# Two expert units computed by token halves during attention, the gate's maximum on TensorE, looser joins, and a decode load issued ahead

## The chip, the cores and the metric

The kernel runs on one NeuronCore of a Trainium2 chip. The metric is device time in microseconds of one launch. Five engines run side by side, each with its own queue in order: PE (TensorE, matmuls into PSUM banks), DVE (VectorE), ACT (ScalarE), POOL (GpSimd) and SP (SyncE, which here only issues DMAs). They meet through semaphores.

## The reference

Attention over 4 batches, 8 heads and 576 positions (four heads with a local window of 32, four with a stride of 32), then a mixture of 8 experts whose gate is normalised over all tokens, then an FFN whose int64 view of float64 weights is decoded on the chip:

```python
x = attention(q, k, v)                       # [2304, 512]: tokens x model
logits = x @ w_gate                          # [2304, 8]
P = np.exp(logits - logits.max())            # one maximum over all tokens and experts
for _ in range(8):                           # Sinkhorn: rows, then columns
    P /= P.sum(1, keepdims=True) + 1e-09
    P /= P.sum(0, keepdims=True) + 1e-09
    P *= N / E
for e in range(8):
    out += P[:, e:e+1] * (np.maximum(x @ w1[e], 0) @ w2[e])
h = out @ w_in
y = (h / (1 + np.exp(-1.702 * h))) @ w_out
```

## The kernel before, in words

Tokens are taken in 3 blocks of 768. A *unit* is one slice of 256 hidden columns of an expert (4 units an expert) or of the FFN (8 units) for one block. There are 120 units in six phases: experts on block 0 (32 units), experts on block 1, FFN on block 0, experts on block 2, FFN on blocks 1 and 2.

Every fp32 operand is split into a high part (ScalarE, `Copy` to fp32r) and a low part (source minus high part, on GpSimd or VectorE), and a product is three matmuls (high·high, high·low, low·high) for each of two 128-row halves of the contraction: six matmuls of 384 columns (line 601). The 2×2 block product of a unit (two token halves of 384, two model halves, two column halves) would be 8 such products; `PRODUCTS` (line 39) does it in 7, with sums of the weights (T1 to T4, made on GpSimd, lines 190 to 192) and of the inputs (S1 to S4, lines 311 to 317). For that the sums of all four input quarters must be there, so both token halves of a block. The results are put together in PSUM banks A, B and C by ScalarE copies (`copy_of`, line 612) and VectorE adds (`add`, line 640; line 658), then `activate` makes the hidden values hh (ScalarE) and hl (VectorE, line 624). `tile_down` multiplies 128 tokens by w2, six matmuls of 512 columns into y (lines 678 to 680), and adds y to the accumulator on VectorE (lines 691 to 707).

The program is a list of *pieces*: 13 a unit, a product and a tile_down in turn (the tile_down is that of the unit before). `side[n]` holds what else is issued after piece n: weight splits, input splits (`plan_inputs`), gate steps, the decode of FFN weights, joins. `advance()` issues the next piece with its side work. All engines' queues are filled in this one order.

The attention comes first, in 48 groups of queries through a pipeline of 52 steps (`att_step`): in step i the groups i-4 (values, line 469), i-3 (transpose, line 451), i-1 (exp) and i (scores, line 400) take their turn, with three gaps a step on PE. In steps 0 to 23 the gaps hold matmuls on zeros (`keep_warm`, line 787; 1.5 a gap on average). Before step 24 the first inputs are put together (`combine`: sum, high, low, all in a row), and from there each gap advances 1.3 pieces (`RATE`). Attention groups write x through VectorE (lines 479, 489).

The probabilities are known only after the whole attention, so the first three experts (`WAITING`) are added up unweighted, stored, and joined later (`plan_kept`, line 721): load at units 14, 17, 20, and six joins of 128 tokens within 18 pieces each. After the attention the gate steps run, one after each piece: logits, maximum over a partition (line 550), maximum over the partitions (`partition_all_reduce` on GpSimd, line 551), exp, 8 Sinkhorn rounds (each with a matmul by ones, line 571). The step behind the last one starts the decode: load (line 259) and 8 VectorE operations (lines 260 to 269) a chunk, 32 chunks spread to unit 60.

What the units of block 0 split is stored to DRAM (s1moe, s2moe) and loaded again for blocks 1 and 2.

Of the kernel before, what the change touches and what calls it, by code (L numbers as in the profile page):

```python
# [15 lines left out]
P = 128  # L16
# [9 lines left out]
NH = 384  # L26
# [6 lines left out]

RATE = 1.3

# [16 lines left out]
def strided_attention_moe_ffn(  # L52
# [130 lines left out]

    def sums_w1(i):

        r = raw[1, i]
        t = rawp.tile([P, 4, 2 * P], F32, tag="sums", name="sums")
# [8 lines left out]
    WHERE = {"W11": (1, 0), "W21": (1, 2), "W22": (1, 3), "T1": (3, 0), "T3": (3, 1), "T2": (3, 2), "T4": (3, 3)}  # L196

    def split_w1(i, k):
        what = PRODUCTS[k][1]
        t = w1p.tile([P, 2, 2 * P], F32R, tag="w1", name="w1")  # L200
        _, kind, blk, n = UNITS[i]
        kept = sw1[kind][n, k].rearrange("p (h c) -> p h c", h=2)
        w1[i, k] = t
        if blk:
            nc.sync.dma_start(out=f(t), in_=kept)
            return
        which, q = WHERE[what]
        src = raw[which, i][:, q, :]
        nc.scalar.activation(out=t[:, 0, :], in_=src, func=AF.Copy)  # L209
        nc.gpsimd.tensor_tensor(out=t[:, 1, :], in0=src, in1=f(t[:, 0, :]), op=ALU.subtract)  # L210
        nc.sync.dma_start(out=kept, in_=f(t))

    def split_w2(i, ft):
        t = w2p.tile([P, 2, D], F32R, tag="w2", name="w2")
        _, kind, blk, n = UNITS[i]
        kept = sw2[kind][n, ft].rearrange("p (h c) -> p h c", h=2)
        w2[i, ft] = t
        if blk:
            nc.sync.dma_start(out=f(t), in_=kept)
            return  # L220
        src = raw[2, i][:, ft, :]
        nc.scalar.activation(out=t[:, 0, :], in_=src, func=AF.Copy)  # L222
        nc.gpsimd.tensor_tensor(out=t[:, 1, :], in0=src, in1=f(t[:, 0, :]), op=ALU.subtract)  # L223
        nc.sync.dma_start(out=kept, in_=f(t))

    def plan_weights():

        for i in range(NU):
            new = [u < NU and UNITS[u][2] == 0 for u in range(i, i + 3)]

            if i + 1 < NU:
# [7 lines left out]
            for ft in range(2):  # L239
                side[piece_at(i, 4 + 2 * ft)].append(lambda i=i, ft=ft: split_w2(i, ft))  # L240
            if new[1]:
                side[piece_at(i, 7)].append(lambda i=i: load_w2(i + 1))


# [74 lines left out]
    def input_of(ph, m):  # L319
        what = PRODUCTS[m][0]  # L320
        return xin[SUMS[what], ph] if what in SUMS else quarters(ph)[what]

    def input_high(ph, m):
        if ph == 0 and not xc:
            xc.update({(0, n): xcp.tile([P, 2, 2, NH], F32R, tag="xc", name="xc") for n in range(NPR)})
        t = xc[0, m] if ph == 0 else xcp.tile([P, 2, 2, NH], F32R, tag="xc", name="xc")
# [6 lines left out]

    def combine(ph, m):

        input_sum(ph, m, nc.vector)
        input_high(ph, m)
        input_low(ph, m, nc.vector)
# [121 lines left out]
    def att_values(i, b, pair, g):  # L460
        eT, U, R, C = att.pop((b, pair, g))
        vt = att_in["v", b, pair]
        if i < NFIRST and i % 2:
            av = ps.tile([P, 512], F32, tag="C", name="av")
        else:
            av = eps.tile([P, 512], F32, tag="pa", name="av")
# [81 lines left out]
    def gate_max():  # L548
        mx = sk[:, 0, 0:1]
        nc.vector.tensor_reduce(out=mx, in_=pr, axis=AX.XY, op=ALU.max)  # L550
        nc.gpsimd.partition_all_reduce(sk[:, 0, 1:2], mx, P, bass.bass_isa.ReduceOp.max)

    def gate_exp():
        ng = sk[:, 0, 2:3]
        nc.vector.tensor_scalar_mul(ng, sk[:, 0, 1:2], -1.0)
        nc.scalar.activation(out=pr, in_=pr, func=AF.Exp, bias=ng)

# [34 lines left out]
    def product(i, k):  # L592
        ph, kind, blk, n = UNITS[i]
        _, _, b, opens, ends = PRODUCTS[k]
        if opens:
            open_bank(b, i)
        o = bank[b][:, :NH]
        w, x = w1.pop((i, k)), xc[ph, k]
        todo = [(kk, hw, hx) for kk in range(2) for hw, hx in ((0, 0), (0, 1), (1, 0))]
        for m, (kk, hw, hx) in enumerate(todo):  # L600
# [110 lines left out]
    def plan_kept():  # L711
# [43 lines left out]
    def unit_pieces(i):  # L755
        out = []
        for k in range(NPR):
            if i < NU:
                def prod(i=i, k=k):
                    r = product_and_after(i, k)  # L760
                    if r is not None:
                        later.append(r)
                out.append(prod)
            if k < TB:
                def down(i=i, k=k):
                    if i > 0:
                        tile_down(i - 1, k)
                    after()
                out.append(down)
        return out  # L770

    for i in range(NU + 1):
        pieces += unit_pieces(i)
# [5 lines left out]
    with tc.manual_schedule():  # L779
# [33 lines left out]

        quota = [0.0]
        ahead = {10 + 2 * k: (lambda k=k: split_w1(0, k)) for k in range(NPR)}
        ahead[9] = lambda: [t() for t in sums_w1(0)]
        load_w1(1)
        first = {13: 3, 17: 0, 22: 6}

        def fill_first():  # L820
            quota[0] += IDLE_GAP
            keep_warm(int(quota[0]))
            quota[0] -= int(quota[0])

        def fill():
            quota[0] += RATE
            while quota[0] >= 1:
                advance()
                quota[0] -= 1

        for i in range(NSTEP):
            if i < NFIRST + 4:
                att_step(i, fill_first)
                if i in ahead:
                    ahead[i]()
                if i in first:
                    combine(0, first[i])
            else:
                if i == NFIRST + 4:
                    combine(0, 1)  # L840
                    combine(0, 2)
                    side[2].append(lambda: combine(0, 4))
                    side[4].append(lambda: combine(0, 5))
                    side[PPU].append(lambda: gate_logits(0))
                att_step(i, fill)
        early.close()
# [92 lines left out]
```

## Time and profile before

| | us |
|---|---|
| three runs | 2064.30 median, 2060.92 to 2064.44 |
| profiled execution, its own time | 2064.13 |
| its span (first to last instruction) | 2062.3 |
| PE busy | 2023.6 (98%) |
| DVE / ACT / POOL busy | 1310.8 / 705.4 / 608.1 |
| mean granted TensorE clock | 0.993 of 2.4 GHz |

A row of the profile gives the line of the kernel, the engine, the operation and output<-inputs. Matmul durations overlap, so the cost of a matmul group is read from its start to the start of what follows. Windows and timelines are in us from the span's start.

### The profile page before, as it was taken

How to read it: one execution, taken by the hardware profiler on the slowest of the kernel's cores; microseconds unless marked ns; L12 is line 12 of the kernel's file. 1: busy time of each engine (PE TensorE's matmuls, PEld its weight loads, DVE VectorE, ACT ScalarE, POOL GpSimd, SP SyncE). 2: the span in 40 equal slices, each digit the busy share in tenths (PEclk: the TensorE clock that was granted, in tenths of full speed). 3: DMA queues.
4: the chain of work that ended last, by engine and by line, in shares of the span. 5: the costliest groups of instructions: out<-in, count | busy, mean ns of one | idle time of the engine just before them, and what ended most of it. 6: DMA issues, size and time to landing. Idle time of an engine off the chain costs nothing.

```text
span 2062.3 us, 30239 instructions
## 1 busy us (share of the span) xinstructions
PE 2023.6 (98%) x10538; PEld 1778.3 (86%) x10538; DVE 1310.8 (64%) x2310; ACT 705.4 (34%) x1735; POOL 608.1 (29%) x609
## 2 busy tenths in 40 slices
PE   9799999999999999999999999999999999999999
PEld 6577878888888888898898888888898889889888
DVE  6766576888778666666665666544554455466656
ACT  5655533443443222222222555222222222333432
POOL 3556656777777000000000667100000000300300
PEclk9899999999999999999999999999999999999999
DMA  5467567888887666666666676655555555655653
GB/s 182 145 217 279 205 237 268 314 305 300 282 289 250 205 206 228 220 213 220 223 209 201 215 244 209 219 180 189 187 179 185 198 177 181 194 180 178 209 190 128
DMA packets 185287, 445.51 MB, mean 216 GB/s; under 512 B 21040, under 2 KB 21168, under 8 KB 184368
## 3 DMA queue, kind: packets, MB, share of 16 engines
q1 hardware_dynamic: 184848, 443.12, 64.3%
q8 instruction: 84, 1.38, 0.3%
q14 instruction: 67, 0.55, 0.1%
q10 hardware_dynamic: 288, 0.46, 0.1%
HBM read 310.33 MB, written 133.17 MB: 215 GB/s over the span
## 4 chain that ended last, share of the span: by engine, by line
PE 87%; DVE 6%; issue 2%; DMA 2%; ACT 1%; POOL 1%; POOLq 0%; ACTq 0%; SPq 0%; DVEq 0%
PE pA L601 22%; PE y L680 15%; PE y L678 15%; PE y L679 15%; PE pC L601 11%; PE pB L601 5%; DMA acc<-kept 1%; PE sc L400 1%; PE idle_out L787 1%; PE av L469 1%; PE pt L451 1%; DVE acc L697 1%; POOL w L210 1%; DVE hl L634 1%; DVE xc L332 1%
## 5 line engine op out<-in xcount | busy, mean ns | idle before, releaser
L697 DVE SCALAR_TENSOR_TENSOR acc<-y,pr,acc 128x512 f32<-128x512 f32 x486 | 364.3, 750 | 445.7 <-PE y L680 443.0
L680 PE MATMUL y<-w,hl 128*128 128x512 f32 x1440 | 573.4, 398 | 5.7 <-DVE hl L624 3.7
L678 PE MATMUL y<-w,hh 128*128 128x512 f32 x1440 | 568.1, 395 | 6.9 <-DVE acc L693 3.8
L679 PE MATMUL y<-w,hh 128*128 128x512 f32 x1440 | 569.3, 395 | 0.0
L601 PE MATMUL pA<-xc,w 128*128 128x384 f32 x2880 | 565.0, 337 | 2.4 <-ACT c L612 1.7
L601 PEld LDWEIGHTS pA<-xc,w 128*128 128x128 f32 x2880 | 513.6, 189 | 37.0 <-ACT c L612 2.1
L680 PEld LDWEIGHTS y<-w,hl 128*128 128x128 f32 x1440 | 270.3, 188 | 68.0 <-DVE hl L624 6.3
L678 PEld LDWEIGHTS y<-w,hh 128*128 128x128 f32 x1440 | 270.8, 188 | 47.8 <-DVE acc L693 4.1
L679 PEld LDWEIGHTS y<-w,hh 128*128 128x128 f32 x1440 | 270.5, 188 | 33.5
L601 PE MATMUL pC<-xc,w 128*128 128x384 f32 x1440 | 294.4, 339 | 0.0
L601 PEld LDWEIGHTS pC<-xc,w 128*128 128x128 f32 x1440 | 258.9, 189 | 21.1 <-issue 0.6
L621 ACT ACTIVATE hh<-pB 128x384 fp32r<-128x384 f32 x192 | 94.5, 492 | 410.8 <-DVE pB L640 238.5
L612 ACT ACTIVATE c<-pA 128x384 f32<-128x384 f32 x240 | 117.6, 490 | 254.6 <-PE pA L601 254.6
L332 POOL TENSOR_TENSOR xc<-z,xc 128x768 fp32r<-128x768 f32 x8 | 15.1, 1891 | 546.0 <-ACT xc L327 546.0
L270 POOL TENSOR_TENSOR x<-x,r 128x512 f32<-128x512 f32 x32 | 41.4, 1294 | 415.7 <-DVE r L269 394.1
L601 PE MATMUL pB<-xc,w 128*128 128x384 f32 x720 | 145.8, 337 | 0.0
L210 POOL TENSOR_TENSOR w<-sums,w 128x256 fp32r<-128x256 f32 x160 | 126.8, 796 | 59.6 <-ACT w L209 52.4
L601 PEld LDWEIGHTS pB<-xc,w 128*128 128x128 f32 x720 | 128.1, 188 | 11.0 <-issue 0.5
L707 DVE TENSOR_TENSOR acc<-y,acc 128x512 f32<-128x512 f32 x126 | 86.4, 686 | 79.1 <-PE y L680 78.8
L223 POOL TENSOR_TENSOR w<-raw,w 128x512 fp32r<-128x512 f32 x80 | 107.1, 1339 | 85.4 <-ACT w L222 85.4
L612 ACT ACTIVATE c<-pC 128x384 f32<-128x384 f32 x120 | 59.0, 492 | 176.6 <-PE pC L601 176.6
L621 ACT ACTIVATE hh<-pC 128x384 fp32r<-128x384 f32 x96 | 47.2, 492 | 180.6 <-DVE pC L640 176.4
(109 smaller groups left out, 1995.7 us busy)
## 6 DMA issues: line engine op xcount, KB each, us to landing
w<-s1moe SPq DMA_DIRECT2D x448, 256.0 KB, 2.7
w<-s2moe SPq DMA_DIRECT2D x128, 512.0 KB, 3.7
s1moe<-w SPq DMA_DIRECT2D x224, 256.0 KB, 3.8
s2moe<-w SPq DMA_DIRECT2D x64, 512.0 KB, 3.8
w<-s1ffn SPq DMA_DIRECT2D x112, 256.0 KB, 2.7
raw<-wa SPq DMA_DIRECT2D x32, 512.0 KB, 4.9
raw<-wb SPq DMA_DIRECT2D x32, 512.0 KB, 5.3
w<-s2ffn SPq DMA_DIRECT2D x32, 512.0 KB, 3.8
```

The costliest lines, as they stand in the source:

```text
L210: nc.gpsimd.tensor_tensor(out=t[:, 1, :], in0=src, in1=f(t[:, 0, :]), op=ALU.subtract)
L223: nc.gpsimd.tensor_tensor(out=t[:, 1, :], in0=src, in1=f(t[:, 0, :]), op=ALU.subtract)
L270: lambda: nc.gpsimd.tensor_tensor(out=x, in0=x, in1=f(r), op=ALU.add),
L332: eng.tensor_tensor(out=t[:, 1], in0=input_of(ph, m), in1=f(t[:, 0]), op=ALU.subtract)
L601: nc.tensor.matmul(out=o, lhsT=w[:, hw, kk * P : (kk + 1) * P], rhs=x[:, hx, kk, :], start=opens and m == 0, stop=ends and m == len(todo) - 1,
L612: nc.scalar.activation(out=t, in_=bank[b][:, :NH], func=AF.Copy)
L621: nc.scalar.activation(out=hh, in_=src, func=AF.Relu)
L678: nc.tensor.matmul(out=y, lhsT=hh[:, c], rhs=w[:, 0], start=(m == 0), stop=False)
L679: nc.tensor.matmul(out=y, lhsT=hh[:, c], rhs=w[:, 1], start=False, stop=False)
L680: nc.tensor.matmul(out=y, lhsT=hl[:, c], rhs=w[:, 0], start=False, stop=(m == 1))
L697: nc.vector.scalar_tensor_tensor(out=a, in0=y, scalar=p, in1=a, op0=ALU.mult, op1=ALU.add)
L707: nc.vector.tensor_tensor(out=a, in0=y, in1=a, op=ALU.add)
```

## The change

1. The first two units (`PLAIN = 2`) take the plain 8 products with unsummed weights and inputs, token half by token half: half 0 of unit 0, half 0 of unit 1, half 1 of unit 0, half 1 of unit 1 (`half_pieces`, 4 products each, and the three tile_downs of the half before). Half 0 needs 384 tokens only. Its 11 pieces are issued from attention step 14 on, 0.4 a gap, one matmul on zeros in a gap without a piece.
2. From step 24 on the rate is 1.15 pieces a gap (1.3 before). Input sums and splits of unit 2 are side work of pieces 12 to 26; the splits of the plain quarters follow steps 10, 13, 22 and 23. Attention groups 6 to 11 are reordered. From group 11 on transposes go to bank `pa`, from group 10 to 19 values to bank B.
3. T1 to T4 of units 0 and 1, which blocks 1 and 2 still read, are made and stored later (`plan_sums`, units 16 to 27).
4. The gate's maximum over partitions: a matmul by the identity, a VectorE maximum, a matmul by ones.
5. Joins: loads at units 14, 19, 24, six joins within 52 pieces each. First decode load 8 pieces ahead of its use.
6. In the last unit before blocks 1 and 2, three low parts of inputs go from VectorE to GpSimd (`low_v`).

```diff
-RATE = 1.3
+RATE_HALF = 0.4
+RATE = 1.15
+PLAIN = 2
...
+        for at, k in zip((10, 12, 14, 16, 18, 19, 21), range(NPR)):
+            side[at].append(lambda k=k: split_w1(PLAIN, k))
+        side[8].append(lambda: [t() for t in sums_w1(PLAIN)])
...
+    def plan_sums(dp, i, lo, hi):
...
+        def split(k):
+            t = dp.tile([P, 2, 2 * P], F32R, tag="kw", name="kw", bufs=2)
+            split_into(t, quarter(i, PRODUCTS[k][1]), sw1["moe"][UNITS[i][3], k].rearrange("p (h c) -> p h c", h=2))
+        tasks = [load, lambda: None, sums] + [lambda n=n: r["todo"][n]() for n in range(4)]
+        tasks += [lambda k=k: split(k) for k in range(NPR) if PRODUCTS[k][1][0] == "T"]
+        spread(tasks, lo, hi)
...
+        side[lo - 8].append(lambda: step(0, 0))
         for i in range(len(todo)):
-            if i == 0:
-                order.append((0, 0))
...
+    def plan_first_sums():
+        v, g = nc.vector, nc.gpsimd
+        for m, at, eng in ((1, 12, g), (2, 17, v), (4, 21, g), (5, 25, v)):
+            side[at].append(lambda m=m: input_sum(0, m, v))
+            side[at + 1].append(lambda m=m, eng=eng: split_input(m, eng))
...
-            low_v = (1, 3, 5) if shared else (0, 3, 6) if PHASES[ph - 1][1] == 0 else ()
+            low_v = (1, 3, 5) if shared else ()
...
-        nc.gpsimd.partition_all_reduce(sk[:, 0, 1:2], mx, P, bass.bass_isa.ReduceOp.max)
+    def gate_max_row():
+        pm = spare_bank([P, 512], "pm")
+        nc.tensor.matmul(out=pm[:1, :P], lhsT=sk[:, 0, 0:1], rhs=ident, start=True, stop=True)
+        nc.vector.tensor_reduce(out=sk[:1, 0, 1:2], in_=pm[:1, :P], axis=AX.X, op=ALU.max)
+    def gate_max_all():
+        pm = spare_bank([P, 512], "pm")
+        nc.tensor.matmul(out=pm[:, :1], lhsT=ones[:1, :], rhs=sk[:1, 0, 1:2], start=True, stop=True)
+        nc.vector.tensor_scalar_mul(sk[:, 0, 2:3], pm[:, :1], -1.0)
...
-        steps += [lambda: None] * 3 + [gate_exp]
+        steps += [lambda: None, gate_max_row, lambda: None, gate_max_all, lambda: None, gate_exp]
...
+    HALVES = [(i, h) for h in range(2) for i in range(PLAIN)]
+    def half_product(n, k):
+        i, h = HALVES[n]
+        col, first = divmod(k, 2)
+        if not first:
+            open_bank("AC"[col], 0)
+        w = w1[i, ("W11", "W12")[col] if first else ("W21", "W22")[col]]
+        x = xc[0, (0, "X21")[h] if first else (3, 6)[h]]
+        o = bank["AC"[col]][:, :NH]
+        sum_of_six(o, w, x, not first, bool(first))
+        if first:
+            return activate(i, f"{h + 1}{col + 1}", o, f"{n % 2 + 1}{col + 1}")
...
-            u = WAITING * UPE + 2 + 3 * e
+            u = WAITING * UPE + 2 + 5 * e
-            spread([lambda e=e, t=t: join(e, t) for t in range(TB)], piece_at(u, 8), piece_at(u + 2, 0))
+            spread([lambda e=e, t=t: join(e, t) for t in range(TB)], piece_at(u, 8), piece_at(u + 4, 8))
...
+        def fill_half():
+            quota[0] += RATE_HALF
+            if quota[0] >= 1 and done[0] < BY_HALF:
+                advance()
+                quota[0] -= 1
+            else:
+                keep_warm(1)
```

Three places where the order moves. First PE in attention steps 17 and 18, before: av are values of a group, pt its transposes, sc scores, idle_out the matmuls on zeros.

```order
L469 MATMUL av<-eT,vt 64x72 x2
L787 MATMUL idle_out<-idle 128x384
L451 MATMUL pt<-cst,e 126x126 x4
L787 MATMUL idle_out<-idle 128x384 x2
L400 MATMUL sc<-qkt 96x128 x4
L787 MATMUL idle_out<-idle 128x384
```

The same place on PE in the changed kernel: pA<-xc,w is one half product, the six y rows are one tile_down.

```order
L515 MATMUL av<-eT,vt 64x72 x2
L657 MATMUL pA<-xc,w_544 128x384 x6
L495 MATMUL pt<-cst,e 126x126 x4
L887 MATMUL idle_out<-idle 128x384
L444 MATMUL sc<-qkt 96x128 x4
L750 MATMUL y<-w_456,hh_659 128x512
L751 MATMUL y<-w_456,hh_659 128x512
L752 MATMUL y<-w_456,hl_660 128x512
L750 MATMUL y<-w_507,hh_737 128x512
L751 MATMUL y<-w_507,hh_737 128x512
L752 MATMUL y<-w_507,hl_738 128x512
```

Of the 30 gaps of steps 14 to 23, 11 hold a piece (8 products, 3 tile_downs) and the others one matmul on zeros; before, each held 1 or 2 of these.

Second, GpSimd at the gate's maximum, before: the all-reduce (sk) stands between the weight splits (L210, L223) and the weight sums (L190) of two units.

```order
L223 TENSOR_TENSOR w_3090<-raw_2898,w_3090 128x512
L210 TENSOR_TENSOR w_3123<-raw_2805,w_3123 128x256
L551 ISA
L551 ISA sk<-sk 128x1
L210 ISA
L210 TENSOR_TENSOR w_3151<-sums,w_3151 128x256
L190 TENSOR_TENSOR sums<-raw_3013 128x512
```

In the changed kernel GpSimd has nothing of the gate, and PE has two small matmuls (pm) instead, a tile_down and a product apart.

```order
L657 MATMUL pA<-xc,w_2785 128x384 x6
L602 MATMUL pm<-cst,sk 1x128
L750 MATMUL y<-w_2773,hh_2900 128x512
L751 MATMUL y<-w_2773,hh_2900 128x512
L752 MATMUL y<-w_2773,hl_2901 128x512
L750 MATMUL y<-w_2804,hh_2846 128x512
L751 MATMUL y<-w_2804,hh_2846 128x512
L752 MATMUL y<-w_2804,hl_2847 128x512
L657 MATMUL pC<-xc,w_2826 128x384 x6
L607 MATMUL pm<-sk,cst 128x1
```

Each pm waits for a VectorE result issued two pieces earlier. Third, SP's queue at the first decode load (w<-wc), before: s1moe and s2moe are stores of split weights, raw are loads of weights.

```order
L174 DMA raw_3638<-wa 128x1024
L211 DMA s1moe<-w_3648 128x512
L224 DMA s2moe<-w_3660 128x1024
L211 DMA s1moe<-w_3678 128x512
L259 DMA w_3682<-wc 128x1024
L224 DMA s2moe<-w_3698 128x1024
```

And in the changed kernel:

```order
L210 DMA s1moe<-w_3453 128x512
L185 DMA raw_3457<-wb 128x1024
L210 DMA s1moe<-w_3484 128x512
L299 DMA w_3518<-wc 128x1024
L210 DMA s1moe<-w_3545 128x512
L210 DMA s1moe<-w_3558 128x512
L210 DMA s1moe<-w_3577 128x512
L178 DMA raw_3581<-wa 128x1024
```

Before, it stood three stores behind the load of a unit's weights (raw<-wa); now it stands four rows ahead of that load.

## Rows read from the trace of the kernel before

**Rows 1.** Windows: length, busy PE, PEld, DVE, ACT, POOL; PEclk, DMA share, GB/s

```profile
41.74:71.33 29.59, 25.85 (x226) 18.50 (x225) 23.79 (x66) 20.51 (x88) 12.68 (x15) 1.00 0.55 181
71.33:102.86 31.53, 22.43 (x149) 17.68 (x149) 20.52 (x35) 17.20 (x53) 17.83 (x20) 0.73 0.41 137
102.86:260.72 157.86, 156.54 (x990) 125.19 (x987) 101.75 (x224) 82.17 (x285) 94.62 (x110) 1.00 0.67 233
260.72:345.00 84.28, 76.49 (x418) 65.47 (x418) 60.14 (x141) 29.19 (x71) 45.37 (x53) 0.98 0.69 237
420.00:520.00 100.00, 95.76 (x469) 83.76 (x468) 85.36 (x122) 39.20 (x97) 75.84 (x76) 1.00 0.85 297
```

**Rows 2.** Timeline, PE, attention steps 21 and 22: start, duration, operation

```profile
62.94 0.49 PE L451 MATMUL pt<-cst,e 96*128 96x96 f32 x4
63.22 0.42 PE L787 MATMUL idle_out<-idle 128*128 128x384 f32 x1
63.56 0.68 PE L400 MATMUL sc<-qkt 64*96 64x128 f32 x8
64.17 0.61 PE L787 MATMUL idle_out<-idle 128*128 128x384 f32 x2
64.71 0.55 PE L469 MATMUL av<-eT,vt 128*64 128x96 f32 x8
65.19 0.44 PE L787 MATMUL idle_out<-idle 128*128 128x384 f32 x1
```

**Rows 3.** Timeline, PE, first pieces; in brackets the wait ahead and its end

```profile
71.81 1.31 PE L601 MATMUL pA<-xc,w 128*128 128x384 f32 x6
78.51 0.87 PE L451 MATMUL pt<-cst,e 96*128 96x96 f32 x4 [5.39 <-DVE x L479]
101.42 1.51 PE L537 MATMUL pl<-x,wgr 128*32 128x192 f32 x32
```

**Rows 4.** Short windows: at the first pieces, and behind the wait for the decode

```profile
72.00:74.00 2.00, 1.13 (x6) 0.81 (x5) 1.24 (x2) 0.73 (x1) 0.00 (x0) 1.00 0.00 0
76.00:78.00 2.00, 0.00 (x0) 0.00 (x0) 1.08 (x3) 1.53 (x3) 0.00 (x0) 0.50 0.00 0
332.00:336.00 4.00, 4.00 (x17) 3.82 (x17) 4.00 (x6) 1.70 (x5) 3.50 (x4) 0.71 0.63 184
```

**Rows 5.** Timeline, DVE, two input sums at the first pieces

```profile
75.02 0.95 DVE L313 TENSOR_TENSOR sb<-sa,x 128x768 f32<-128x768 f32 x1
86.24 3.70 DVE L317 TENSOR_TENSOR sb<-x,sb 128x768 f32<-128x768 f32 x1
```

**Rows 6.** Timeline, PE, pieces just behind the attention

```profile
257.22 1.23 PE L601 MATMUL pC<-xc,w 128*128 128x384 f32 x6
258.29 0.39 PE L678 MATMUL y<-w,hh 128*128 128x512 f32 x1
259.68 1.21 PE L601 MATMUL pA<-xc,w 128*128 128x384 f32 x6
```

**Rows 7.** Timelines of POOL, ACT, PE and DVE in the gate steps

```profile
282.06 0.73 POOL L210 TENSOR_TENSOR w<-sums,w 128x256 fp32r<-128x256 f32 x1 [6.81 <-issue]
284.19 0.42 ACT L209 ACTIVATE w<-sums 128x256 fp32r<-128x256 f32 x1 [7.23 <-POOL sums L190]
286.31 1.31 PE L601 MATMUL pA<-xc,w 128*128 128x384 f32 x6 [1.69 <-ACT c L612]
328.80 0.43 DVE L260 TENSOR_SCALAR u<-w 128x512 uint32<-128x512 uint32 x1 [6.90 <-DMA s1moe<-w]
329.88 0.50 PE L678 MATMUL y<-w,hh 128*128 128x512 f32 x1 [3.79 <-DVE acc L693]
```

**Rows 8.** Lines: busy, mean ns of one, idle before and its end

```profile
L721 DVE SCALAR_TENSOR_TENSOR acc<-acc,pr 128x512 f32<-128x512 f32 x18 | 20.5, 1137 | 1.4 <-DMA acc<-kept 1.3
L210 POOL TENSOR_TENSOR w<-sums,w 128x256 fp32r<-128x256 f32 x160 | 126.8, 796 | 59.6 <-ACT w L209 52.4 <-issue 6.8
L190 POOL TENSOR_TENSOR sums<-raw 128x512 f32<-128x512 f32 x40 | 53.9, 1347 | 6.0 <-DMA raw<-wa 4.4
```

More of the change, by code (lines that the diff above doesn't have):

```diff
@@ L194, in sums_w1, with quarter, split_into, split_plain @@
         ]
-    WHERE = {"W11": (1, 0), "W21": (1, 2), "W22": (1, 3), "T1": (3, 0), "T3": (3, 1), "T2": (3, 2), "T4": (3, 3)}
+    WHERE = {"W11": (1, 0), "W12": (1, 1), "W21": (1, 2), "W22": (1, 3), "T1": (3, 0), "T3": (3, 1), "T2": (3, 2), "T4": (3, 3)}
+    def quarter(i, what):
+        which, q = WHERE[what]
+        return raw[which, i][:, q, :]
+    def split_into(t, src, kept):
+        nc.scalar.activation(out=t[:, 0, :], in_=src, func=AF.Copy)
+        nc.gpsimd.tensor_tensor(out=t[:, 1, :], in0=src, in1=f(t[:, 0, :]), op=ALU.subtract)
+        if kept is not None:
+            nc.sync.dma_start(out=kept, in_=f(t))
+    def split_plain(i, what):
+        t = w1p.tile([P, 2, 2 * P], F32R, tag="w1", name="w1")
+        w1[i, what] = t
+        ks = [k for k in range(NPR) if PRODUCTS[k][1] == what]
+        kept = sw1["moe"][UNITS[i][3], ks[0]].rearrange("p (h c) -> p h c", h=2) if ks else None
+        split_into(t, quarter(i, what), kept)
     def split_w1(i, k):
@@ L206, in split_w1 @@
             return
[L207 to L211, printed above, removed]
+        src = quarter(i, what)
+        split_into(t, src, kept)
     def split_w2(i, ft):
@@ L221, in split_w2 @@
         src = raw[2, i][:, ft, :]
[L222 to L224 removed]
+        split_into(t, src, kept)
     def plan_weights():
[L228 removed]
+        for at, k in zip((10, 12, 14, 16, 18, 19, 21), range(NPR)):
+            side[at].append(lambda k=k: split_w1(PLAIN, k))
+        side[8].append(lambda: [t() for t in sums_w1(PLAIN)])
+        for i in range(PLAIN - 1, NU):
             new = [u < NU and UNITS[u][2] == 0 for u in range(i, i + 3)]
[L231 removed]
+            if PLAIN <= i < NU - 1:
                 if new[1]:
@@ L238, in plan_weights @@
                 side[piece_at(i, 2)].append(lambda i=i: load_w1(i + 2))
-            for ft in range(2):
+            for ft in range(2 if i >= PLAIN else 0):
                 side[piece_at(i, 4 + 2 * ft)].append(lambda i=i, ft=ft: split_w2(i, ft))
@@ L242, in plan_weights, with load, sums @@
                 side[piece_at(i, 7)].append(lambda i=i: load_w2(i + 1))
+    def plan_sums(dp, i, lo, hi):
+        r = {}
+        def load():
+            r["raw"] = dp.tile([P, 4, 2 * P], F32, tag="raws", name="raws")
+            nc.sync.dma_start(out=r["raw"].rearrange("p q c -> p (q c)"), in_=wa[UNITS[i][3]])
+        def sums():
+            raw[1, i] = r["raw"]
+            r["todo"] = sums_w1(i, dp)
+        def split(k):
[4 more added lines that the diff above has]
+        spread(tasks, lo, hi)
     CHUNK = 512
@@ L319, in input_of @@
     def input_of(ph, m):
-        what = PRODUCTS[m][0]
+        what = PRODUCTS[m][0] if m in range(NPR) else m
         return xin[SUMS[what], ph] if what in SUMS else quarters(ph)[what]
@@ L324, in input_high @@
         if ph == 0 and not xc:
-            xc.update({(0, n): xcp.tile([P, 2, 2, NH], F32R, tag="xc", name="xc") for n in range(NPR)})
+            xc.update({(0, n): xcp.tile([P, 2, 2, NH], F32R, tag="xc", name="xc") for n in ["X21", *range(NPR)]})
         t = xc[0, m] if ph == 0 else xcp.tile([P, 2, 2, NH], F32R, tag="xc", name="xc")
@@ L462, in att_values @@
         vt = att_in["v", b, pair]
-        if i < NFIRST and i % 2:
+        if i < NALONE - 1 and i % 2:
             av = ps.tile([P, 512], F32, tag="C", name="av")
+        elif NALONE - 1 <= i < NFIRST:
+            av = ps.tile([P, 512], F32, tag="B", name="av")
         else:
@@ L596, in product, with sum_of_six @@
             open_bank(b, i)
-        o = bank[b][:, :NH]
-        w, x = w1.pop((i, k)), xc[ph, k]
+        sum_of_six(bank[b][:, :NH], w1.pop((i, k)), xc[ph, k], opens, ends)
+    def sum_of_six(o, w, x, opens, ends):
         todo = [(kk, hw, hx) for kk in range(2) for hw, hx in ((0, 0), (0, 1), (1, 0))]
@@ L760, in prod @@
                     r = product_and_after(i, k)
+                    if i == PLAIN and k == 0:
+                        after()
                     if r is not None:
@@ L765, in down @@
                 def down(i=i, k=k):
-                    if i > 0:
+                    if i > PLAIN:
                         tile_down(i - 1, k)
+                    elif k < TB // 2:
+                        tile_down(i - 1, TB // 2 + k)
                     after()
@@ L770, in unit_pieces, with half_pieces, prod, down @@
         return out
-    for i in range(NU + 1):
+    def half_pieces(n):
+        out = []
+        for k in range(4):
+            def prod(n=n, k=k):
+                r = half_product(n, k)
+                if k == 0:
+                    after()
+                if r is not None:
+                    later.append(r)
+                if n == 0:
+                    after()
+            out.append(prod)
+            if k < TB // 2 and n:
+                def down(n=n, k=k):
+                    i, h = HALVES[n - 1]
+                    tile_down(i, h * (TB // 2) + k)
+                    after()
+                out.append(down)
+        return out
+    for n in range(2 * PLAIN):
+        pieces += half_pieces(n)
+    pieces += [after] * (PLAIN * PPU - len(pieces))
+    for i in range(PLAIN, NU + 1):
         pieces += unit_pieces(i)
@@ L814, in strided_attention_moe_ffn @@
         quota = [0.0]
-        ahead = {10 + 2 * k: (lambda k=k: split_w1(0, k)) for k in range(NPR)}
-        ahead[9] = lambda: [t() for t in sums_w1(0)]
         load_w1(1)
-        first = {13: 3, 17: 0, 22: 6}
+        ahead = defaultdict(list)
+        QUARTERS = ("W21", "W11", "W22", "W12")
+        for n, what in enumerate(QUARTERS):
+            ahead[5 + 2 * n].append(lambda what=what: split_plain(0, what))
+            ahead[12 + n].append(lambda what=what: split_plain(1, what))
+        for ft in range(2):
+            ahead[10 + ft].append(lambda ft=ft: split_w2(0, ft))
+            ahead[17 + ft].append(lambda ft=ft: split_w2(1, ft))
+        ahead[12].append(lambda: load_w1(2))
+        ahead[12].append(lambda: load_w2(1))
+        ahead[10].append(lambda: split_input(3))
+        ahead[NHALF + 3].append(lambda: split_input(0))
+        ahead[22].append(lambda: split_input(6))
+        ahead[NFIRST + 3].append(lambda: split_input("X21"))
+        BY_HALF = 4 * PLAIN + 3 * (PLAIN - 1)
         def fill_first():
@@ L829, in fill @@
                 quota[0] -= 1
+        plan_first_sums()
+        side[20].append(lambda: gate_logits(0))
         for i in range(NSTEP):
[L832 to L845, printed above, removed]
+            if i == NHALF + 4:
+                quota[0] = 0.0
+            att_step(i, fill_first if i < NHALF + 4 else fill_half if i < NFIRST + 4 else fill)
+            for t in ahead.pop(i, ()):
+                t()
+        while done[0] // PPU % 2 or done[0] % PPU < 2:
+            advance()
         early.close()
@@ L855, in strided_attention_moe_ffn @@
         plan_decode(dp, g + len(steps), piece_at(FIRST_UNIT[2] - 4, 0))
+        for i in range(PLAIN):
+            plan_sums(dp, i, piece_at(WAITING * UPE + 4 + 6 * i, 0), piece_at(WAITING * UPE + 9 + 6 * i, 0))
         while done[0] < len(pieces):
```

31 lines of the change are left out of this document (15 added, 16 removed).

## The prediction

> **What bounds the kernel now.** I read the windows of the whole span first, and then, where a window is short of PE work, PE's timeline there and the timelines of the engines that PE waits for. From 103 us on PE is busy nearly all the time: 156.54 of 157.86 us while attention and pieces are mixed. Behind that, time can only be saved by removing PE work or one of the few idle spots. The spots are [rows 1]: 9.1 us idle in 71.33 to 102.86, together with a granted clock of 0.73; 7.8 us idle in the gate steps (260.72 to 345); 4.2 us in 420 to 520, where the joins are. Ahead of these stands 41.74 to 71.33 (attention steps 14 to 23), where PE is full, but of matmuls on zeros. The change touches all four places and adds two products (16 instead of 14 in units 0 and 1).
>
> I call the stretches B (steps 14 to 23), C (step 24 to piece 107), D (gate and first decode) and E (joins). The order on PE up to step 14 is that of before, so B starts at 41.7 again; what ScalarE and GpSimd split earlier there hides under steps whose ScalarE is not full (20.51 of 29.59 in the next ten steps).
>
> **Prices.** From start to next start: a transpose group 0.28, scores 0.61, values 0.48, one zero matmul 0.34, two 0.54 [rows 2]; a product 1.07, a tile_down 1.39 [rows 6].
>
> **B.** Before: 29.59. Now: ten steps of attention at 1.37 are 13.7; 19 zero matmuls at 0.34 are 6.5; 8 products and 3 tile_downs are 8.6 + 4.2. Sum 33.0. Waits were 3.7 (29.59 less 25.85); with relu, low parts and adds also in ScalarE's and VectorE's queues I take 5.6, so 38.6: **+9.0**.
>
> **C.** Before, 71.33 to 260.72 is 189.4. Its second part is the measure for a mixed stretch: 157.86 us for 51 products, 44 tile_downs, 21 scores, 24 values, 23 transposes [rows 1], switches included. Now from step 24 to piece 107 there are 52 products, 40 tile_downs, 24 scores, 28 values, 27 transposes and one gate_logits (1.5, [rows 3]). The difference: +1.1, −5.6, +1.8, +1.9, +1.1, +1.5, so +1.9 before rounding, and 159.8. What goes is the start of before: there the first product stood alone, and then PE waited 5.39 us for a transpose whose bank hung on VectorE [rows 3], since VectorE did sum, low part, sum, low part in a row; the clock fell to half, 1.2 GHz, in that pause [rows 4]. What is late next: VectorE. It gets the four sums and two low parts of unit 2 within pieces 12 to 26, some 6 us at 0.95 each over four steps. It was busy 101.75 of 157.86 in the mixed part; here that rises by a quarter, and a sum can take 3.70 instead of 0.95 when GpSimd is at work [rows 5]. The lower rate also means fewer gaps with two pieces, thus less cover for a transpose that waits for the copy out of its bank. Bounds for these added waits: nothing (every sum is issued at least one piece ahead of its product), and 16, about what the old start lost (31.53 less some 15 of work at full clock: 8 products, one gate_logits, 3 scores, 4 values and 4 transposes). I take 6, nearer to the lower end, since the sums are now single and pieces apart. So C is 165.8: **−23.6**.
>
> Behind piece 107 stand one product and one tile_down more than behind piece 109 before: **+2.4**. Start in all: **−12.2**.
>
> **D.** After the all-reduce GpSimd stood idle for 6.81; ScalarE waited 7.23 for weight sums behind it, and PE 1.69 for a ScalarE copy [rows 7]. With the maximum on PE this chain goes: −1.7. VectorE stood 6.90 at the first decode operation, whose load had only just been issued, and PE 3.79 for an add behind it [rows 7]; eight pieces ahead are some 9.8 us at the prices above, more than the 6.90: −3.8. Behind that wait the clock was 0.71 for 4 us [rows 4] and lower than 1 just before: −1.7. The other 2.3 us of D's idle are Sinkhorn matmuls waiting for VectorE, which was behind after the first stall; I take a quarter as gone, −0.6. The new matmuls each wait for a VectorE result issued two pieces earlier, as the Sinkhorn ones do: +0.6 (bounds 0 and 2). Sum **−7.2**; bounds −9 and −1.5.
>
> **E.** Of 4.2 us idle I leave 1: a join every 8.7 pieces instead of every 3 on a VectorE busy 85.36 of 100. Against it, T1 to T4 of two units come on top of GpSimd's 75.84 of 100 in units 16 to 27: per unit three sums (1.35, and two half as large, taken at 0.80) and four splits of 0.80 [rows 8], 6.2 us in five units, on top of 11.8 a unit; the sums and splits of running units have most of a unit of slack. +0.2. Sum **−3.0**; bounds −4.2 and +2.
>
> A rule speaks against this term. A join takes 1137 ns in the mean [rows 8], against 0.95 us for a larger sum of two inputs when undisturbed [rows 5]. The Trainium skill (SBUF — State Buffer, section Who interferes with whom) says that a VectorE operation with two inputs in SBUF and a GpSimd operation lock each other out for a whole instruction, whichever came first. The 3.70 in [rows 5] agrees. By the rule alone each of the 14 added GpSimd operations could hold a join or a decode operation for its length; that is the rival "joins" below, priced from rows.
>
> The three low parts that move from VectorE to GpSimd before blocks 1 and 2 count nothing: GpSimd splits no w1 there (those weights are loaded), and the xc they make are read a unit later. Cover gone, it would cost a few tenths.
>
> **Sum.** 2064.1 (profiled execution, 2062.3 span and 1.8 around it; the median of the runs, 2064.3, is the same) −12.2 −7.2 −3.0 = 2041.7, so **2042**. The likeliest case's own range is 2035 to 2050.
>
> **Rivals.**
> - *VectorE carries the start* (0.18): C's added waits are 16 rather than 6, because the sums collide with GpSimd splits as in [rows 5]. For: the 3.70. Against: in B VectorE had 5.8 us free. Time: 2042 + 10 = 2052.
> - *Gate waits move* (0.12): the maximum's two matmuls and the Sinkhorn rounds wait on PE, D gives 1.5 only: 2047.
> - *Joins* (0.10): the spread joins and the decode are held by the added GpSimd work, E at +2 instead of −3: 2047.
> - *No added waits at all* (0.12): B at 3.7, C at 0, D −9, E −4.2: 2042 − 1.9 − 6 − 1.8 − 1.2, some 2031 to 2033.
> - *The clock falls* (0.06, slower): with fewer zero matmuls PE pauses in steps 14 to 26 as it did at [rows 3], and the granted clock stays where it was in 71.33 to 102.86, at 0.73, for B and the half pieces in C, some 38.6 + 25 us. Price: 64 × (1/0.73 − 1) = 24, and 3 for the pauses: 2069. It decides if the mean clock there is below about 0.75; at 0.85 the result is still faster. Against: in B before, with PE idle 3.7 of 29.59 us in short waits, the clock was 1.00 [rows 1].
>
> The forecast has 0.42. **Range** for 8 in 10: 2032 to 2057, from no added waits to the start and one more term lost. What measurement can tell from no change is about 0.2%, 4 us: faster than 2060 has 0.89 (all but the last rival and the tails where several meet), within 0.05, slower 0.06.
>
> **What would show it.** B ends near 80 us with PE busy over 85% and clock 1.00; no PE wait above 2 us between 80 and 105; the last values of the attention near 240. No GpSimd pause of 6.8 us and no VectorE wait of 6.9 us in the gate steps; in units 14 to 28 PE idle about 1 us, joins near 1 us each. Wrong if PE shows a wait of several us at pieces 11 to 26 or in front of pm, if the clock in B is well under 1, or if the attention ends later than 250.

## The result, and the profile after

The changed kernel took 2029.69 us (median of 4 runs, 2027.98 to 2031.72), the kernel before 2062.86 beside it; the ratio is 0.9840, with a 95% interval of 0.9823 to 0.9857. So 33 us went, where 22 were forecast (2042, range 2032 to 2057): the sign was right, the size too small, and the time lies below the range.

The first rows are windows of the changed kernel, with the columns of [rows 1]: steps 14 to 23 (B), step 24 to piece 107 (C), the gate steps and first decode (D), a stretch of the joins (E), and the end of the FFN units on block 0.

```profile
40.98:76.09 35.11, 33.84 (x266) 25.88 (x266) 26.38 (x71) 21.30 (x89) 16.27 (x19) 1.00 0.54 191
76.09:242.60 166.51, 160.93 (x1070) 125.69 (x1069) 112.36 (x245) 90.70 (x318) 101.14 (x113) 1.00 0.61 215
243.70:317.50 73.80, 71.71 (x409) 62.11 (x409) 58.20 (x138) 27.50 (x68) 44.10 (x50) 1.00 0.72 253
393.00:493.00 100.00, 100.00 (x499) 89.43 (x498) 81.13 (x123) 43.23 (x107) 83.71 (x88) 1.00 0.90 313
1241.00:1271.00 30.00, 28.94 (x142) 25.06 (x141) 21.16 (x30) 15.73 (x30) 29.04 (x17) 1.00 0.63 209
```

The clock is 1.00 in all five, where [rows 1] had 0.73 and 0.98. The joins' stretch is full and holds 499 matmuls instead of 469. Next is PE's timeline at the start and in the gate steps (start, duration, operation, the wait ahead); it answers [rows 3] and the PE rows of [rows 7].

```profile
42.65 1.34 PE L657 MATMUL pA<-xc,w 128*128 128x384 f32 x6
44.86 0.55 PE L515 MATMUL av<-eT,vt 128*64 128x96 f32 x8 [0.86 <-DVE eT L499]
79.79 0.51 PE L752 MATMUL y<-w,hl 128*128 128x512 f32 x1 [0.74 <-DVE hl L696]
100.75 0.62 PE L495 MATMUL pt<-cst,e 126*126 126x126 f32 x4 [1.02 <-DVE x L525]
239.56 0.55 PE L515 MATMUL av<-eT,vt 128*64 128x96 f32 x8
253.54 0.38 PE L602 MATMUL pm<-cst,sk 128*1 128x128 f32 x2 [0.20 <-DVE hl L696]
256.85 0.35 PE L607 MATMUL pm<-sk,cst 1*128 1x1 f32 x2 [0.28 <-DVE hl L696]
296.88 0.39 PE L626 MATMUL pc<-sk,cst 128*128 128x8 f32 x2 [0.98 <-DVE sk L622]
```

The first product stands at 42.65, 29 us earlier than in [rows 3]; the 5.39 us wait is gone and up to 106 us none above 1.02 us has come in its place (the longest of the whole stretch C is 1.30 us, at 124.15); the maximum's two matmuls wait 0.48 us together. A join, by the line that answers to [rows 8], takes 1064 ns instead of 1137:

```profile
L793 DVE SCALAR_TENSOR_TENSOR acc<-acc,pr 128x512 f32<-128x512 f32 x18 | 19.1, 1064 | 1.3 <-DMA acc<-kept 1.2
```

To see where the 34.7 us between the two profiled executions went, the start of the same tile_down is read in both traces, counted from 0 through the kernel (its first matmul is L678 before, L750 after):

| tile_down | before | after | gained | gained since the row above |
|---|---|---|---|---|
| 45, just behind the mixed stretch | 266.3 | 250.7 | 15.6 | 15.6 (start: B, C and behind) |
| 68, behind the first decode | 339.9 | 316.6 | 23.4 | 7.8 (gate and decode) |
| 196, behind the joins | 681.2 | 652.4 | 28.9 | 5.5 (joins) |
| 420, start of the last FFN unit on block 0 | 1273.1 | 1244.2 | 28.9 | 0 |
| 434 | 1316.9 | 1282.2 | 34.8 | 5.9 |
| 719 | 2056.9 | 2022.2 | 34.7 | 0 |

(At tile_down 44 only 14.2 are gained, because the changed kernel has one of the gate's logits steps, 1.4 us at 245.13, ahead of it and the kernel before, at 262.20, behind it; at 45 both have the same work behind them.) The fifth row is the surprise: 5.9 us in 40, where I had counted nothing. The kernel before has this there: a window, PE's waits, the three low parts on VectorE, and three GpSimd rows beside them.

```profile
1290.00:1302.00 12.00, 9.42 (x32) 7.41 (x31) 9.17 (x10) 4.59 (x9) 6.53 (x4) 0.72 0.49 167
1275.80 0.51 PE L680 MATMUL y<-w,hl 128*128 128x512 f32 x1 [1.35 <-DVE hl L634]
1293.38 0.71 PE L678 MATMUL y<-w,hh 128*128 128x512 f32 x1 [2.06 <-ACT hh L631]
1295.04 0.79 PE L680 MATMUL y<-w,hl 128*128 128x512 f32 x1 [0.52 <-DVE hl L634]
1273.02 1.66 DVE L332 TENSOR_TENSOR xc<-x,xc 128x768 fp32r<-128x768 f32 x1
1281.82 2.55 DVE L332 TENSOR_TENSOR xc<-x,xc 128x768 fp32r<-128x768 f32 x1
1294.91 2.57 DVE L332 TENSOR_TENSOR xc<-x,xc 128x768 fp32r<-128x768 f32 x1
1272.01 1.85 POOL L313 TENSOR_TENSOR sb<-sa,x 128x768 f32<-128x768 f32 x1
1281.71 1.84 POOL L332 TENSOR_TENSOR xc<-sb,xc 128x768 fp32r<-128x768 f32 x1
1294.65 2.01 POOL L313 TENSOR_TENSOR sb<-sa,z 128x768 f32<-128x768 f32 x1
```

PE waits for hh and hl, and in the FFN both need a product that VectorE makes from the sigmoid (line 630), in the same queue as these low parts.

After, the low parts are on GpSimd, and PE has two short waits left:

```profile
1261.53 0.51 PE L750 MATMUL y<-w,hh 128*128 128x512 f32 x1 [0.65 <-ACT hh L703]
1262.69 0.50 PE L752 MATMUL y<-w,hl 128*128 128x512 f32 x1 [0.42 <-DVE hl L706]
```

The waits fell from 3.93 to 1.07 us; and a clock of 0.72 over 12 us is an estimated 3.4 us of lost work. Together that is 6.2, against 5.9 measured.

### The profile page after: what moved, and what is told of

It reads as the page before. It is cut to its first block, busy times and chain, and to the rows that moved or that the text cites. A ratio compares the mean times of both kernels' runs of the same rounds, so it can differ in the third digit from the quotient of the medians.

```text
span 2027.5 us, 30190 instructions
## 1 busy us (share of the span) xinstructions
PE 2007.1 (99%) x10528; PEld 1766.7 (87%) x10528; DVE 1304.5 (64%) x2298; ACT 704.0 (35%) x1732; POOL 626.9 (31%) x618
## 4 chain that ended last, share of the span: by engine, by line
PE 91%; DVE 5%; ACT 1%; DMA 1%; POOL 1%; issue 1%; SPq 0%; POOLq 0%; ACTq 0%; DVEq 0%
PE pA L657 23%; PE y L752 16%; PE y L751 15%; PE y L750 15%; PE pC L657 12%; PE pB L657 6%; PE sc L444 1%; PE av L515 1%; PE pt L495 1%; PE idle_out L887 1%; DVE hl L696 1%; POOL w L208 1%; DVE hl L706 0%; DMA acc<-kept 0%; PE px L810 0%
## 5 line engine op out<-in xcount | busy, mean ns | idle before, releaser
L750 PE MATMUL y<-w,hh 128*128 128x512 f32 x1440 | 566.3, 393 | 1.1 <-ACT hh L703 1.0
L750 PEld LDWEIGHTS y<-w,hh 128*128 128x128 f32 x1440 | 270.5, 188 | 40.4 <-ACT hh L703 2.6
L208 POOL TENSOR_TENSOR w<-raw,w 128x256 fp32r<-128x256 f32 (+1 forms) x202 | 203.5, 1015 | 110.9 <-ACT w L207 95.3
L208 POOL TENSOR_TENSOR w<-sums,w 128x256 fp32r<-128x256 f32 x152 | 120.2, 795 | 39.8 <-ACT w L207 39.5
```

The lines of the kernel that those rows point to most:

```text
L750: nc.tensor.matmul(out=y, lhsT=hh[:, c], rhs=w[:, 0], start=(m == 0), stop=False)
```

## Experiments

All times are medians beside runs of the kernel before (2062.64, 2062.35 and 2061.86 in the three sessions). "Changed" is the changed kernel, 2029.69.

| kernel | us | ratio to before, 95% | against changed |
|---|---|---|---|
| changed, low parts back | 2039.52 | 0.9873 to 0.9902 | +9.8 |
| changed, all-reduce back | 2033.03 | 0.9849 to 0.9882 | +3.3 |
| changed, decode load not ahead | 2037.39 | 0.9863 to 0.9892 | +7.7 |
| changed, tight joins | 2036.10 | 0.9856 to 0.9886 | +6.4 |
| before, low parts moved | 2056.26 | 0.9961 to 0.9982 | |
| before, all but the new start | 2042.94 | 0.9897 to 0.9924 | +13.3 |
| changed, seven low parts on VectorE | 2040.46 | 0.9883 to 0.9911 | +10.8 |
| changed, fourth low part on VectorE | 2033.85 | 0.9847 to 0.9877 | +4.2 |
| changed, seventh low part on VectorE | 2033.79 | 0.9846 to 0.9875 | +4.1 |
| changed, no zero matmuls from the first product on | 2028.67 | 0.9827 to 0.9857 | −1.0 |
| also fewer before that | 2029.62 | 0.9825 to 0.9855 | −0.1 |
| also a third of them | 2029.27 | 0.9829 to 0.9862 | −0.4 |

Traces of kernels with the same code up to tile_down 44 differ there by up to 3.5 us (of eight such traces the changed kernel's own is the earliest, by 1.4); so a part is read below between two tile_downs near it, beside the median.

**Low parts back, and low parts alone.** Two kernels: the changed one with this line as before, and the kernel before with it as changed.

```
-            low_v = (1, 3, 5) if shared else ()
+            low_v = (1, 3, 5) if shared else (0, 3, 6) if PHASES[ph - 1][1] == 0 else ()
```

> The changed kernel with three low parts of inputs back on VectorE before the phases that follow a block-0 phase. Theory (the moved low parts are what removed the stall at the end of the FFN on block 0): 5.8 us over the changed kernel, about 2035.5, with PE waits of about 3.9 us there and the granted clock at one half for some 7 us; nothing at the end of the first expert phase. Rival (the stall went because everything before it stands at another time, and the low parts count nothing, as predicted): 2029.7, at most 1 us more, and no such waits.

> The kernel before with one edit: the three low parts of phases 1 and 3 that VectorE took are given to GpSimd. Theory (the edit that I counted as nothing ends a pause of TensorE at the end of the FFN on block 0): 2062.8 less 5.9, so about 2057, with no wait of TensorE above 0.7 us and a clock of 1.00 in the 30 us before the next unit, and no gain elsewhere. Rival (the gain there comes only with the other parts of the change, since the stages before it are shifted): 2061 to 2064.

Measured: +9.8 and −6.1. Between tile_downs 420 and 434 the first loses 6.1 us in the trace; another 2.7 go at 180 to 190, the end of phase 0 (experts on block 0), where I expected nothing. The second gains 5.9 at 420 to 434, only 0.2 at 180 to 190, and stays within 0.8 of the kernel before up to tile_down 420. Why the parts cost 2.7 at 180 to 190 in the changed kernel alone stays open. The window that answers to 1270 to 1300, first with the parts back:

```profile
1246.00:1276.00 30.00, 25.69 (x113) 21.84 (x112) 23.07 (x29) 13.97 (x26) 23.22 (x14) 0.89 0.48 162
```

and then in the kernel before with the parts moved:

```profile
1270.00:1300.00 30.00, 28.92 (x143) 25.05 (x142) 21.15 (x30) 15.62 (x30) 28.95 (x17) 1.00 0.64 209
```

The code of this stretch is otherwise the same; 30 matmuls and the clock make the difference. That the edit counts nothing is refuted from both sides, and so is that its gain needs the other parts.

**Why three parts cost so much.** Three variants of that line in the changed kernel: all seven parts, the fourth alone, the seventh alone.

```
+            low_v = (1, 3, 5) if shared else range(NPR) if PHASES[ph - 1][1] == 0 else ()
+            low_v = (1, 3, 5) if shared else (3,) if PHASES[ph - 1][1] == 0 else ()
+            low_v = (1, 3, 5) if shared else (6,) if PHASES[ph - 1][1] == 0 else ()
```

> The changed kernel with all seven low parts of phases 1 and 3 on VectorE and none on GpSimd. Theory (a low part on VectorE is slow, 2.55 us against 0.95, because GpSimd works on the others in the same microseconds): VectorE's low parts fall to about 1.0 to 1.3 us each and the kernel takes 0 to 4 longer than the changed one. Rival (any such part on VectorE holds up the hl chain behind it, whoever works beside it): more than the 9.8 that three low parts on VectorE cost.

> The changed kernel with one low part of phases 1 and 3 on VectorE, that of the fourth product (the one that took 2.55 us at 1281.82 in the kernel before, ahead of the 2.06 us wait of TensorE); the other six are on GpSimd. Theory (it is the slow part that stands ahead of a waiting sigmoid chain that costs): most of the 9.8 of three parts, so 2033 to 2037, with the pause and the half clock near tile 426. Rival (it is VectorE's load over the whole unit): a third, so 2032 to 2033, and the same for the next kernel.

> The same with the low part of the seventh product alone on VectorE (2.57 us at 1294.91 before, behind the long wait). Theory: it stands behind the waits, so 2029.5 to 2031. Rival (load over the unit): 2032 to 2033, as for the kernel with the fourth.

With seven, three of the parts near 1250 to 1273 fell to 0.96 us, but four took 1.42 to 2.29, and the kernel was the slowest of these: my 0 to 4 was wrong, and the rival's "more than the 9.8" came out, though by 0.9 us only. Its timeline shows a part beside an idle GpSimd, one beside a sum that GpSimd makes, and the wait of PE behind them:

```profile
1254.80 0.96 DVE L371 TENSOR_TENSOR xc<-sa,xc 128x768 fp32r<-128x768 f32 x1 [0.43 <-ACT xc L366]
1255.90 1.86 POOL L354 TENSOR_TENSOR sa<-x 128x768 f32<-128x768 f32 x1 [3.76 <-DVE xc L371]
1256.27 2.29 DVE L371 TENSOR_TENSOR xc<-sb,xc 128x768 fp32r<-128x768 f32 x1
1271.72 0.50 PE L750 MATMUL y<-w,hh 128*128 128x512 f32 x1 [2.60 <-ACT hh L703]
```

The GpSimd sum ends at 1257.76, and VectorE's part ends 0.80 us later: as if held until then. That is the lock of the Trainium skill (SBUF — State Buffer, section Who interferes with whom), and the trace agrees with it: all four slow parts of this trace, and all three of the kernel before above, end 0.80 to 0.82 us after a GpSimd row, and the three of 0.96 us ran beside an idle GpSimd. But taking GpSimd's low parts away helped only in part: GpSimd still makes the sums, and the seven parts together take 9.70 us of VectorE, where the three took 6.77.

The single parts fit neither theory. The fourth's time lies in its theory's range, but without the pause and the half clock; and its part took 1.23 us in this trace, not 2.55, so a slow fourth part was not what ran. The seventh is above its theory's 2029.5 to 2031. What the rival said came out in one point: both cost the same. Their medians fit "a third each, or a little more", but between tile_downs 420 and 434 their traces lose only 0.7 and 1.2 us, where three parts lose 6.1 and seven 5.4 (at 180 to 190 it is 1.7 and 1.7 against 2.7 and 3.8); of the fourth's 5.9 against the changed trace, 3.9 stand before tile_down 64, where the code is that of the changed kernel.

The fourth's part, then windows of the kernels with the fourth, with the seventh and with all seven parts:

```profile
1256.64 1.23 DVE L371 TENSOR_TENSOR xc<-x,xc 128x768 fp32r<-128x768 f32 x1
1246.00:1276.00 30.00, 28.22 (x138) 24.35 (x137) 21.89 (x30) 15.68 (x30) 28.14 (x16) 1.00 0.62 209
```
```profile
1246.00:1276.00 30.00, 27.95 (x135) 23.72 (x134) 22.48 (x30) 14.29 (x27) 24.88 (x14) 1.00 0.63 207
```
```profile
1246.00:1276.00 30.00, 25.34 (x116) 21.58 (x115) 24.87 (x34) 15.01 (x28) 17.39 (x11) 0.94 0.49 167
```

The clock stays at 1.00 with one part and falls with three (0.89 above) and with seven (0.94), which is an estimated 3.3 and 1.8 us of work in 30. Without it the fourth part, the seventh, the three and the seven lose 0.7, 1.2, 2.8 and 3.6 us, and they take 1.23, 2.58, 6.77 and 9.70 us on VectorE. So the cost is not a sum over parts: in these four traces the loss grows with the time that the parts take on VectorE, and the clock comes on top only in the two where PE paused for 2 us and more here. How much of that time the lock adds, what the first part alone costs, and which two of the three suffice, was not tried.

**All-reduce back.** GpSimd takes the gate's maximum again.

```
-        pm = spare_bank([P, 512], "pm")
-        nc.tensor.matmul(out=pm[:1, :P], lhsT=sk[:, 0, 0:1], rhs=ident, start=True, stop=True)
...
+        nc.gpsimd.partition_all_reduce(sk[:, 0, 1:2], mx, P, bass.bass_isa.ReduceOp.max)
```

> The changed kernel with the gate's maximum over partitions by the GpSimd all-reduce again. Theory (the pause behind the all-reduce also delays the Sinkhorn rounds): about 3.5 us more than the changed kernel, 2033, with a GpSimd pause of about 6.8 us and PE waits of 3 us or more until the first Sinkhorn rounds are done. Rival (only the one PE wait of 1.7 us is the price, as predicted, and the two matmuls cost 0.6): 2031.

Measured: +3.3, as the theory had it; +2.9 in the trace at tile_downs 44 to 68. GpSimd pauses ahead of the all-reduce and behind it, and ScalarE and PE wait behind that, as in [rows 7]:

```profile
261.43 0.38 POOL L600 PARTITION_ALL_REDUCE sk<-sk  x1 [5.82 <-issue]
268.97 0.73 POOL L208 TENSOR_TENSOR w<-raw,w 128x256 fp32r<-128x256 f32 x1 [7.16 <-issue]
271.80 0.42 ACT L207 ACTIVATE w<-sums 128x256 fp32r<-128x256 f32 x1 [8.28 <-POOL sums L194]
273.91 1.31 PE L651 MATMUL pA<-xc,w 128*128 128x384 f32 x6 [1.26 <-ACT c L677]
```

**Decode load not ahead.** The first unit's decode load is issued with its first step again.

```
-        side[lo - 8].append(lambda: step(0, 0))
+            if i == 0:
+                order.append((0, 0))
```

> The changed kernel with the first decode load issued with the first decode step again. Theory: VectorE waits about 6.9 us for it, PE about 3.8, and the clock falls for a few us: 5.7 us more, about 2035.4. Rival (the load is early enough in the new order of SP's queue, so the load ahead is worth nothing): 2030, VectorE wait under 2 us.

Measured: +7.7, more than the theory's 5.7; +7.5 in the trace at tile_downs 60 to 68. VectorE's wait (the row names the load; the one in [rows 7] names a store), PE's, and a window behind them:

```profile
315.10 0.43 DVE L300 TENSOR_SCALAR u<-w 128x512 uint32<-128x512 uint32 x1 [7.22 <-DMA w<-wc]
316.05 4.21 PE L658 MATMUL pA<-xc,w 128*128 128x384 f32 x12 [4.51 <-DVE pB L731]
316.05:325.00 8.95, 8.95 (x33) 8.27 (x34) 6.33 (x11) 3.85 (x10) 6.22 (x7) 0.69 0.35 96
```

The pause is 4.51, and a clock of 0.69 over the 8.95 us behind it is an estimated 2.8 more: 7.3.

**Tight joins.** The joins of a block stand within two units again.

```
-            u = WAITING * UPE + 2 + 5 * e
+            u = WAITING * UPE + 2 + 3 * e
...
-            spread([lambda e=e, t=t: join(e, t) for t in range(TB)], piece_at(u, 8), piece_at(u + 4, 8))
+            spread([lambda e=e, t=t: join(e, t) for t in range(TB)], piece_at(u, 8), piece_at(u + 2, 0))
```

> The changed kernel with the joins as before: six within 18 pieces, loads at units 14, 17, 20. Theory (the idle time of PE shown for the joins leaves out what each pause costs when matmuls start again, so that they cost more than their 4.2 us of idle): about 5.5 us more than the changed kernel, 2035. Rival (the price is the idle time, less what is left of it, as predicted): 3.0 us, about 2032.7; with the added weight sums on GpSimd either may be 1 us more.

Measured: +6.4 by the medians, nearer the theory; the trace has +4.7 at tile_downs 68 to 196, between the two. A window of it and the joins' line:

```profile
393.00:493.00 100.00, 96.91 (x478) 85.20 (x477) 87.24 (x124) 41.23 (x102) 83.25 (x86) 1.00 0.91 325
```
```profile
L793 DVE SCALAR_TENSOR_TENSOR acc<-acc,pr 128x512 f32<-128x512 f32 x18 | 20.5, 1139 | 0.8 <-DMA acc<-kept 0.6
```

PE is idle 3.1 us there, yet 21 matmuls fewer than after fit into the 100 us, at 0.2 us each 4.2.

**All but the start.** The kernel before with every edit but the new start; its diff is the change's own without that part.

> The kernel before with all of the change but the new start: gate maximum by matmuls, decode load ahead, low parts on GpSimd, spread joins. Theory (the parts add): 9.3 of gate and decode, 5.5 of the joins and 5.9 of the low parts make 20.7, so 2042, and the new start alone is worth the rest, 12 to 14. Rival (the parts overlap, as the four kernels with one part undone lose 27.2 in sum by themselves without the start): between 2035 and 2039, so that the start is worth 6 to 9 only.

Measured: 2042.94, which the theory had at 2042. In the trace gate and decode give 7.0 (tile_downs 44 to 68), the joins 6.9 (72 to 196), the low parts 5.9. The start alone is then worth 13.3 by the medians. That the four kernels with one part undone lose 27.2 in sum, against some 20 gained here, is no contradiction: the low parts undone also cost 2.7 at the end of phase 0, where moving them in the kernel before gains 0.2, and gate and decode undone cost 11.0 by the medians, where they give 7.0 here. What a part is worth depends on what else has been changed. Its window at the start repeats the second of [rows 1], so the clock's fall there belongs to the old start:

```profile
71.33:102.86 31.53, 22.41 (x143) 17.64 (x142) 20.88 (x36) 16.44 (x49) 17.63 (x20) 0.73 0.39 127
```

**Fewer zero matmuls.** Three kernels: none from the first product on (step 14; the expectations call it step 10, by its group; 69 left of 88 in the trace), then also one per gap before that (48), then one in every second gap (27).

```
             if quota[0] >= 1 and done[0] < BY_HALF:
                 advance()
                 quota[0] -= 1
-            else:
-                keep_warm(1)
...
-IDLE_GAP = 1.5
+IDLE_GAP = 1.0
...
+IDLE_GAP = 0.5
```

> The changed kernel without the matmuls on zeros that the start's planner sets into gaps. Theory (they stand where TensorE had nothing else, but each takes its place ahead of work that may come earlier): 2 to 6 below the changed kernel with the clock at 1.00 in the stretch 40 to 245. Rival (they keep the clock): the granted clock falls to 0.50 behind a gap in that stretch, and the kernel takes 10 or more longer than the changed one.

> The changed kernel without zero matmuls from step 10 of the attention on, and with one in each gap of the steps before in place of one or two in turn. Theory (they stand in TensorE's way there: 42 gaps, half of them with a second zero matmul of 0.2): 2 to 4 below the changed kernel. Rival (VectorE, busy 27.31 of the 35.15 us there, or the clock sets the pace): no change, or a clock of 0.50 in the first 45 us and up to 5 longer.

> The same with a zero matmul in every second gap only. Theory: another 2 to 4 less, as far as VectorE's 27.31 us allow (at most 8 below the changed kernel in all). Rival: the clock falls to half in the first 45 us, and the kernel is slower than the changed one.

Measured: −1.0, −0.1 and −0.4, within the runs' spread: neither the gain I expected nor a loss. The same window of the first and of the changed kernel, in this order:

```profile
71.33:102.86 31.53, 27.98 (x216) 21.52 (x215) 22.72 (x48) 16.76 (x57) 16.22 (x16) 1.00 0.36 125
```
```profile
71.33:102.86 31.53, 29.16 (x223) 22.16 (x223) 22.54 (x47) 17.38 (x61) 15.80 (x17) 1.00 0.37 130
```

PE is less busy and no quicker, and the clock holds at 1.00. In the third kernel the clock does fall, with PE busy throughout:

```profile
37.00:47.50 10.50, 10.50 (x64) 7.66 (x61) 8.60 (x20) 7.23 (x30) 6.67 (x8) 0.51 0.72 250
```

and its tile_down 44 still comes no later than the changed kernel's (246.0 for 246.6), so the half clock cost no time there that shows. None of the three beats the changed kernel by more than can be measured.

## Why the prediction was too small

**The step that failed** is "The three low parts that move from VectorE to GpSimd ... count nothing ... Cover gone, it would cost a few tenths." It asked whether GpSimd had room for them, and not what VectorE lost by having them. Shown, added to the kernel before and taken from the changed one: 6 us at the end of the FFN units on block 0. The rows stood in the trace of before: the prediction's list of idle spots ends at 520 us and leaves out the waits of 1.35, 2.06 and 0.52 us and the clock of 0.72 there. A window of all of 1200 to 1400 is busy for 196.07 of 200 us and hides them; PE's waits at the place of the edit show them. This is the largest of the four differences summed up below.

**The start** was forecast at −12.2 and came to −15.6 in the two traces, −13.3 by the medians. B took 35.1 for 38.6: its work 33.84 for 33.0, but its waits 1.3 for 5.6. C took 166.5 for 165.8: idle 5.6 for 6, the work 1 more than priced. So the mechanism and the choice between the bounds 0 and 16 held in C; B's waits were the mis-sized term. Another 0.8 is that step 14 begins at 40.98 for 41.74, which is less than such traces differ by. The seven other traces with this start gain 12.0 to 14.2 at tile_down 45, so part of the 15.6 is the luck of one trace; by the medians the miss is 1.1.

**Gate and decode** were forecast at −7.2 and gave 7.8 in the traces, 7.0 with the old start: right together. Undone one by one they cost more than forecast: the gate 2.9 to 3.3 for 1.7, the decode 7.5 to 7.7 for 5.5, of the kind forecast, wait plus clock.

**The joins** were forecast at −3.0 with a lower bound of −4.2, the idle time. They gave 5.5 in the traces, 6.9 with the old start, and 6.4 (4.7 in the trace) when undone. The bound was the mistake: 4.2 us idle in [rows 1] stood for 30 matmuls less in the 100 us, at 0.2 us each 6.0. PE's busy time does not show all that a pause costs.

With these four as the two traces have them, 2041.7 − 5.9 − 3.4 − 0.6 − 2.5 gives 2029.3.

**The rivals.** *VectorE carries the start* fell: no PE wait above 1.02 us in 80 to 105. *Gate waits move* fell: 0.48 us in front of the maximum's matmuls. *Joins*, the rival that the Trainium skill's lock stands beside, fell although GpSimd is busier (83.71 for 75.84 of 100): a join is shorter, 1064 ns. The lock shows at the low parts instead. *The clock falls* fell: it is 1.00 in B and C, and stayed so without the zero matmuls of B. *No added waits*, at 2031 to 2033, was the nearest in time but not in cause, since C did have its waits (5.6 us).

## What to carry to other kernels

When an edit takes work off an engine, look at what waits for that engine at the places where the work stood, in the trace of before, however small the work is. Price a pause of the bounding engine by the work that a window lacks (matmuls counted) and add the clock behind it; idle time alone was too little by a quarter to a half in the places checked here. An edit that was only argued to be free deserves the cheapest experiment: undo it alone.

## What the runs showed of the hardware

- One low part of 128x768 on VectorE took 0.96 us beside an idle GpSimd and up to 2.58 beside one that was reading and writing tiles; the seven slow ones read above ended 0.80 to 0.82 us after a GpSimd operation did.
- Around a pause of PE of 2.06 us the granted clock stood at 0.72 over 12 us, and behind one of 4.51 us at 0.69 over 8.95 us; two waits of under 1 us in 30 us left it at 1.00. Around one of 1.80 us it was 1.00 with the low parts back (610 to 625 us) and 0.76 with seven on VectorE (614 to 621 us).
- With the all-reduce back GpSimd shows no work for 5.82 us ahead of it and for 7.16 us behind it; its own row is 0.38 us long. The profile names nothing that GpSimd waited for in either gap, so whether it was still at work behind the row is not shown.
